# Attention with pooled keys and values: each batch's v is asked for two tiles later than its k, and one constant earlier

## The chip, the cores and the metric

One core of a Trainium2 chip runs the whole program. The metric is the device time of one execution in microseconds (us), as the median of several runs; the kernel before has 1315.34 us (three runs, 1312.93 to 1316.71). Its profiled execution took 1315.6 us, of which 1313.8 us lie between the first and the last instruction (the span).

## The reference, cut to what matters

```
def _attn_ref(q, k, v):            # 8 batches, 8 heads, 576 positions, 64 wide
    k_p = k.reshape(B, H, Sp, 8, D).mean(axis=3)      # 72 pooled keys
    v_p = v.reshape(B, H, Sp, 8, D).mean(axis=3)      # 72 pooled values
    scores = scale * np.matmul(q, k_p.transpose(0, 1, 3, 2))
    attn = exp(scores - max) / (sum + 1e-09)
    return np.matmul(attn, v_p)

x = attn_out as 4608 tokens of 512
x = _moe_ref(x, w_skip, w_gate, w1, w2)    # each token kept or sent to one of 8 experts
return _moe2_ref(x, w_in, w_out)           # (h * sigmoid(h)) @ w_out, h = x @ w_in
```

## The kernel before

The program has three stages one behind the other: the attention (up to about 150 us of the span, its last tiles up to about 175 us), the mixture of experts, and two large matmuls with a gate. The change touches the attention alone.

**Tiles.** The 4608 tokens are worked off in 36 tiles of 128. Two batches share nine tiles: `first = [0, 4, 9, 13, 18, 22, 27, 31]` is the first tile of each batch. The loop over `i` runs a software pipeline: in turn `i` it takes the scores of tile `i+2` (`s` on PE, their maximum `mx` on DVE, their exponentials `prb` on ACT), transposes those of tile `i+1` (`pt` on PE, copied to `pts` on ACT), multiplies tile `i` with the values (`pv` on PE) and divides by the sums (`post` on DVE: `sm`, `cc`, `x`, `lg`). Each finished tile `x` is written to HBM by one transfer `xa<-x`. The tiles `x` lie in a ring of four, so that the `x` of tile 7 must wait until the write of tile 3 has landed. The product `pv` has one buffer, so that the next `pv` waits until DVE has written `x`.

**What a batch needs.** Three transfers bring it: q and k (1152 KB each) and v (1200 KB, 120 partitions by 2560 numbers). DVE pools k (`kp`), ACT spreads it (`kbd`). POOL pools v in three additions, two into `v` itself and a third into `vp`, and spreads `vp` into `vex`. PE transposes `vp` (`vtp`, in `router1`), ACT copies that to `vt`, PE multiplies it with the router's weights (`cps`, in `router2`), and DVE puts the result into `vex`. For batch b+1 POOL is asked to begin two turns ahead of the batch b before it (`i + 2 == first[b]`), and `router1` stands three turns further on.

**Order.** Nothing is scheduled by a planner: each engine works its instructions in the order in which the code is written. All loads and all `xa` writes are issued by SP, in that order, on one hardware queue; SP stops at each write until DVE has finished the tile. The loads of batch b+2 are written in turn `first[b] - 2`:

```
if i + 2 == first[b]:
    if 0 < b < B - 1:
        loadq(b + 1)
        pool_k(b + 1, nc.vector, (0,))
        pool_v(b + 1)
    if b + 2 < B:
        loadk(b + 2)
        loadv(b + 2)
```

**The triangle's constants.** `constb` (64 KB) is loaded by SP in turn 2; in turn 6 `consts()` converts it on ACT to `trib`, which the routing needs.

A wrapper records every operation, so that nearly all rows of the profile name its line, L110; the operations are told apart by their tiles.

Of the kernel before, what the change touches and what calls it, by code (L numbers as in the profile page):

```python
# [18 lines left out]
P = 128  # L19
B, H, S, D = 8, 8, 576, 64  # L20
# [32 lines left out]
C_E, C_MV, C_LID, C_WT, C_THR, C_LE, C_UN, C_PK, C_TRI = 0, 2, 13, 49, 57, 153, 217, 241, 265  # L53
# [99 lines left out]
class Kern:  # L153
# [19 lines left out]
    def attention(self, xa, rs, extra):  # L173
        nc, tc, c = self.nc, self.tc, self.c
        self.todo = todo = []
        self.slow = iter(())
        with tc.tile_pool(name="as", bufs=1) as s1, \
# [11 lines left out]
            def loadk(b):  # L189
                k_t[b] = s2.tile([P, 4, G, POOL], F32, name=f"k{b}", tag="k")  # L190
                nc.sync.dma_start(k_t[b].rearrange("p a g t -> p a (g t)"), self.kT[b])

            def loadv(b):
                v_t[b] = s2.tile([P, NC, POOL, D], F32, name=f"v{b}", tag="v")
                for c in (slice(0, ON0), slice(ON0, NC)) if b == 0 else (slice(NC),):
                    nc.sync.dma_start(v_t[b][:CP, c].rearrange("p c t d -> p c (t d)"), self.vR[b][:, c])

            def loadq(b):
                q_t[b] = s2.tile([P, 4, S], F32, name=f"q{b}", tag="q", bufs=3)
                nc.sync.dma_start(q_t[b], self.qT[b])  # L200
# [15 lines left out]
            def pool_v(b, on_dve=0):  # L216

                v, g, n = v_t.pop(b), nc.gpsimd, on_dve
                vp = st[b, "v"] = s2.tile([P, NC, D], F32, name=f"vp_{b}", tag="vp")
                if n:  # L220
                    nc.vector.tensor_reduce(vp[:CP, 0:n], v[:CP, 0:n].rearrange("p c t d -> p c d t"), AX.X, ALU.add)
                v, vp = v[:CP, n:], vp[:CP, n:]
                g.tensor_tensor(v[:, :, 0:4], v[:, :, 0:4], v[:, :, 4:8], ALU.add)
                g.tensor_tensor(v[:, :, 0:2], v[:, :, 0:2], v[:, :, 2:4], ALU.add)
                g.tensor_tensor(vp, v[:, :, 0], v[:, :, 1], ALU.add)

            def values(b):
                vp, ve = st[b, "v"], vex[b % NB]
                for i, (h0, n) in enumerate(HEADS):
                    j = HOFF[i]  # L230
                    nc.gpsimd.tensor_tensor(ve[:CP, j:j + n, 0:D], bc(vp[:CP, i], 1, n),
                                            bc(mv[:CP, j:j + n], 2, D), ALU.mult)

            def keys(b):
                kp, kb = st.pop((b, "k")), kbd[b % NB]
                for j in range(2):
                    nc.scalar.mul(kb[:, :, j, :], kp, c[:, C_E + j:C_E + j + 1])

            def router1(b):
                vpf = st[b, "v"].rearrange("p c d -> p (c d)")  # L240
                ps = self.hp.tile([P, 512], F32, name=f"vtp_{b}", tag="hp")
                nc.tensor.transpose(ps[:, 0:CP], vpf[:CP, 0:128], self.ident[:CP, :CP])
                nc.tensor.transpose(ps[:, CP:2 * CP], vpf[:CP, 128:256], self.ident[:CP, :CP])
                nc.tensor.transpose(ps[:D, 2 * CP:3 * CP], vpf[:CP, 256:320], self.ident[:CP, :CP])
                vt = s2.tile([P, 3, CP], F32, name=f"vt_{b}", tag="vt")
                nc.scalar.copy(vt[:D, 2], ps[:D, 2 * CP:3 * CP])
                nc.scalar.copy(vt[:, 0:2].rearrange("p a b -> p (a b)"), ps[:, 0:2 * CP])
                st[b, "t"] = vt
# [17 lines left out]
            def scores(t):  # L266
                pr = prb[t % 2]
                mx = s2.tile([P, H], F32, name=f"mx_{t}", tag="mx")
                pss = []
                for a in range(2):  # L270
                    ps = self.hp.tile([P, 512], F32, name=f"s_{t}{a}", tag="hp")
                    for b, o, r, m in parts(t):
                        for hp in range(2):
                            nc.tensor.matmul(ps[r:r + m, 144 * hp:144 * hp + 144], q_t[b][:, 2 * a + hp, o:o + m],
                                             kbd[b % NB][:, 2 * a + hp].rearrange("p a g -> p (a g)"),
                                             start=True, stop=True)
                    nc.vector.tensor_reduce(mx[:, 4 * a:4 * a + 4],
                                            ps[:, 0:288].rearrange("p (h g) -> p h g", g=G), AX.X, ALU.max,
                                            negate=True)
                    for h in range(4):  # L280
                        nc.scalar.activation(pr[:, G * (4 * a + h):G * (4 * a + h + 1)], ps[:, G * h:G * (h + 1)],
                                             AF.Exp, bias=mx[:, 4 * a + h:4 * a + h + 1])
                return pr

            def ptrans(t, pr):
                pt = s2.tile([P, NC, P], F32, name=f"pts_{t}", tag="pts")
                for c0, n in ((0, 3), (3, 2)):
                    ps = pp.tile([P, 512], F32, name=f"pt_{t}{c0}", tag="pt", bufs=2)
                    for i in range(n):
                        nc.tensor.transpose(ps[:CP, P * i:P * (i + 1)], pr[:, CP * (c0 + i):CP * (c0 + i + 1)],  # L290
                                            self.ident)
                    nc.scalar.copy(pt[:CP, c0:c0 + n].rearrange("p c n -> p (c n)"), ps[:CP, 0:n * P])
                return pt
# [37 lines left out]
            first = [9 * (b // 2) + 4 * (b % 2) for b in range(B)]  # L331
# [27 lines left out]
            for i in range(-2, NTILE):  # L359
                if i + 2 < NTILE and i != -1:  # L360
                    prs[i + 2] = scores(i + 2)
                ready = todo.pop(0) if todo and i < NTILE - 1 else None
                if ready and ready[0]:
                    ready[0]()
                if i == -2:
                    pool_v(0, ON0)
                    values(0)
                    loadv(1)
                    loadq(1)
                if 0 <= i + 1 < NTILE:  # L370
                    pts[i + 1] = ptrans(i + 1, prs.pop(i + 1))
                if i == -1:
                    router1(0)
                    prs[1] = scores(1)
                    router2(0)
                    pool_k(1, nc.vector, (0,))
                    pool_v(1, ON1)
                    values(1)
                if i >= 0:
                    pv(i, pts.pop(i))  # L380
                a = ready[1]() if ready and ready[1] else iter(())
                b = post(i) if i >= 0 else iter(())
                for _ in range(ready[2] if ready and i < NTILE - 2 else 0):
                    next(a, None)
                for _ in b:
                    next(a, None)
                for _ in a:
                    pass
                for _ in range(SLOW):
                    next(self.slow, None)  # L390
                if i == 0:
                    pool_k(1, nc.vector, (2,))
                    keys(1)
                for b in range(B):
# [4 lines that stand above are left out]
                            pool_v(b + 1)  # L399
                        if b + 2 < B:  # L400
                            loadk(b + 2)
                            loadv(b + 2)
                    if i + 2 == first[b] + 3 + (b == 0) and b + 1 < B:
                        router1(b + 1)
                    if i + 2 == first[b] + 1 and 0 < b < B - 1:
                        pool_k(b + 1, nc.vector, (2,))
                    if i + 2 == first[b] + 2 and 0 < b < B - 1:
                        keys(b + 1)
                    if i + 2 == first[b] + 3 and 0 < b < B - 1:
                        values(b + 1)  # L410
                    if i + 2 == first[b] + 5 and b + 1 < B:
                        router2(b + 1)
                if i == 2:
                    nc.sync.dma_start(self.cb, self.con[:, P + C_TRI:])
                if i == 6:
                    self.consts()
                self.place(2 if i < 27 else 5)
                extra(i)
# [1148 lines left out]
```

## Time and profile before

| | |
|---|---|
| median of three runs | 1315.34 us |
| the profiled execution | 1315.6 us |
| its span | 1313.8 us |
| busy in the span | PE 1261.8 us (96%), DVE 852.6 (65%), ACT 569.2 (43%), POOL 358.0 (27%) |
| mean granted TensorE clock | 0.993 of full speed |
| DMA over the span | 233.77 MB, mean 178 GB/s |
| queue q1 (SP's and ACT's transfers) | 49.0% of 16 engines' span |

Busy shares are averages over three stages that differ. PE is busy nearly throughout from about 220 us on; in the attention it has gaps, and there the DMA engines are the busiest part.

### The profile page before, as it was taken

The numbers are of one execution on the slowest core, as the hardware profiler recorded it, in microseconds if no ns is written. First come the engines' busy times: TensorE is split into PE (matmuls) and PEld (weight loads), VectorE is DVE, ScalarE is ACT, GpSimd is POOL, SyncE is SP. The second block draws the span as 40 slices with busy tenths as digits, with TensorE's granted clock in tenths as the row PEclk, the third lists the DMA queues.
The fourth block names the chain that finished last, engine by engine and source line by source line (L and its number), as shares of the span: only waits on it lengthen the run. The fifth ranks groups of instructions, "written<-read, shape, count | busy, mean of one in ns | idle before, by whom it ended". The sixth has DMA issues, their size and how long they took to land.

```text
span 1313.8 us, 20408 instructions
## 1 busy us (share of the span) xinstructions
PE 1261.8 (96%) x6501; PEld 1075.2 (82%) x6502; DVE 852.6 (65%) x1553; ACT 569.2 (43%) x1188; POOL 358.0 (27%) x312
## 2 busy tenths in 40 slices
PE   6899689999989999999999999999999999999998
PEld 5788677988979898878888888788888888888887
DVE  5788676667667677779733325565784657847565
ACT  4576633454445454344433334534353333533321
POOL 4477433222123220322457503101011010111100
PEclk9999999999999999999999999999999999999999
DMA  9989535656556552248845322634356352463532
GB/s 289 295 271 275 189 126 198 201 179 201 179 190 213 198 188 84 91 167 277 296 155 211 140 93 89 224 129 167 123 183 214 137 177 94 163 210 127 176 109 92
DMA packets 94106, 233.77 MB, mean 178 GB/s; under 512 B 15068, under 2 KB 26972, under 8 KB 90375
## 3 DMA queue, kind: packets, MB, share of 16 engines
q1 hardware_dynamic: 86735, 215.82, 49.0%
q0 software_dynamic: 7008, 16.80, 3.9%
q8 instruction: 42, 0.69, 0.2%
q14 instruction: 33, 0.27, 0.1%
q10 hardware_dynamic: 288, 0.20, 0.0%
HBM read 182.58 MB, written 52.89 MB: 179 GB/s over the span
## 4 chain that ended last, share of the span: by engine, by line
PE 57%; DVE 3%; ACT 1%; issue 1%; POOL 0%; DMA 0%; DVEq 0%; ACTq 0%; POOLq 0%
PE yb L110 20%; PE ps L110 17%; PE fh L110 9%; PE fop L110 9%; PE yp L110 1%; DVE fr L110 1%; DVE ft L110 1%; PE fxp L110 0%; DVE raw L110 0%; PE sx L110 0%; DVE fgl L110 0%; DVE fsg L110 0%; DVE w2l L110 0%; ACT g L110 0%; PE hp L110 0%
## 5 line engine op out<-in xcount | busy, mean ns | idle before, releaser
L110 PE MATMUL yb<-wout,g 128*128 128x512 f32 x1152 | 268.4, 391 | 0.5 <-DMA wout<-wdo 0.4
L110 PEld LDWEIGHTS yb<-wout,g 128*128 128x128 f32 x1152 | 215.0, 188 | 45.5 <-DMA wout<-wdo 0.8
L110 POOL TENSOR_TENSOR tm<-tm,tm 128x512 f32<-128x512 f32 x24 | 32.2, 1340 | 411.9 <-ACT tm L110 411.9
L110 DVE TENSOR_TENSOR yacc<-yb,yacc 128x512 f32<-128x512 f32 x168 | 116.0, 691 | 38.4 <-PE yb L110 31.3
L110 ACT COPY tm<-ps 128x512 f32<-128x512 f32 x72 | 42.3, 588 | 146.3 <-PE ps L110 144.5
L110 PE MATMUL yp<-w2h,hh 128*128 128x512 f32 x240 | 96.4, 402 | 1.8 <-issue 0.9
L110 PE MATMUL yp<-w2l,hh 128*128 128x512 f32 x240 | 94.2, 392 | 2.2 <-DVE w2l L110 2.2
L110 PE MATMUL yp<-w2h,hl 128*128 128x512 f32 x240 | 94.4, 393 | 0.0
L110 ACT CAST g<-sg 128x512 fp32r<-128x512 f32 x96 | 59.6, 621 | 76.8 <-DVE sg L110 76.8
L110 ACT ACTIVATE hh<-hp 128x256 fp32r<-128x256 f32 (+2 forms) x96 | 41.1, 428 | 116.9 <-PE hp L110 105.8
L110 DVE TENSOR_TENSOR fsg<-fh,fsg 128x512 f32<-128x512 f32 x48 | 33.0, 688 | 80.9 <-ACT fsg L110 80.9
L110 ACT ACTIVATE prb<-s,mx 128x72 f32<-128x72 f32 x288 | 65.2, 343 | 45.7 <-DVE mx L110 44.7
L110 PE MATMUL fh<-w1l,fh 128*128 128x512 f32 x336 | 83.4, 390 | 0.0
L110 DVE TENSOR_TENSOR tm<-ps,tm 128x512 f32<-128x512 f32 x24 | 16.6, 691 | 98.1 <-PE ps L110 98.1
L110 PE MATMUL hp<-xtl,w1h 128*128 128x256 f32 (+2 forms) x384 | 71.9, 306 | 3.9 <-DVE xtl L110 3.6
L110 PE MATMUL hp<-xth,w1h 128*128 128x256 f32 (+2 forms) x384 | 71.1, 306 | 4.5 <-issue 1.7
L110 PEld LDWEIGHTS fh<-w1l,fh 128*128 128x128 f32 x336 | 62.8, 188 | 12.9
L110 DVE SCALAR_TENSOR_TENSOR hl<-hp,hh 128x256 fp32r<-128x256 f32 (+2 forms) x96 | 45.9, 478 | 39.8 <-ACT hh L110 33.1
L110 PE MATMUL hp<-xth,w1l 128*128 128x256 f32 (+2 forms) x384 | 69.7, 303 | 0.0
L110 DVE TENSOR_TENSOR g<-sg,g 128x512 fp32r<-128x512 f32 x96 | 65.7, 686 | 5.3 <-ACT g L110 4.7
L110 DVE TENSOR_TENSOR w2l<-raw,w2h 128x512 fp32r<-128x512 f32 x96 | 65.9, 692 | 3.2
L110 ACT ACTIVATE fsg<-fh 128x512 f32<-128x512 f32 x48 | 28.8, 599 | 88.3 <-PE fh L110 88.3
(230 smaller groups left out, 2780.0 us busy)
## 6 DMA issues: line engine op xcount, KB each, us to landing
raw<-w SPq DMA_DIRECT2D x88, 512.0 KB
wout<-wdo SPq DMA_DIRECT2D x48, 512.0 KB
win<-wdi SPq DMA_DIRECT2D x36, 512.0 KB
w1l<-wdi SPq DMA_DIRECT2D x36, 512.0 KB
xa<-x SPq DMA_DIRECT2D x36, 256.0 KB
fx<-xa SPq DMA_DIRECT2D x9, 1024.0 KB
v<-vR SPq DMA_DIRECT2D x7, 1200.0 KB
fr<-w_in SPq DMA_DIRECT2D x16, 512.0 KB
```

Of the source, the lines that this page charges most:

```text
L110: ins = f(*a, **k)
```

## The change

The load of v of batch b+2 moves out of the turn `first[b] - 2`, in which k's load stays, to the turn `first[b]`. For batch 2 that is a move from turn -2 to turn 0. Batches 0 and 1 are loaded ahead of the loop or in turn -2 as before. The load of `constb` moves from turn 2 to turn -2, behind the load of q of batch 1 and ahead of that of k of batch 2. No instruction is added or removed.

```
                     values(0)
                     loadv(1)
                     loadq(1)
+                    nc.sync.dma_start(self.cb, self.con[:, P + C_TRI:])
                 if 0 <= i + 1 < NTILE:
...
                         if b + 2 < B:
                             loadk(b + 2)
-                            loadv(b + 2)
+                    if i + 2 == first[b] + 2 and b + 2 < B:
+                        loadv(b + 2)
                     if i + 2 == first[b] + 3 + (b == 0) and b + 1 < B:
                         router1(b + 1)
...
-                if i == 2:
-                    nc.sync.dma_start(self.cb, self.con[:, P + C_TRI:])
                 if i == 6:
                     self.consts()
```

The first place is SP's list from the load of q of batch 1 (`q_180`) to the last write ahead of batch 3's q (`q_630`). `k_182` and `v_184` are batch 2, `q_374` is q of batch 2, `k_382` and `v_384` are batch 3; the number behind a tile is a buffer's. Before:

```order
L110 DMA q_180<-qT 128x2304
L110 DMA k_182<-kT 128x2304
L110 DMA v_184<-vR 120x2560
L110 DMA xa<-x_84 128x512 x3
L110 DMA q_374<-qT 128x2304
L110 DMA k_382<-kT 128x2304
L110 DMA v_384<-vR 120x2560
L110 DMA constb<-con 128x128
L110 DMA xa<-x_84 128x512 x5
```

And of the change (batch 2 is now `k_183` and `v_284`, its q `q_375`, batch 3 `k_383` and `v_477`):

```order
L110 DMA q_180<-qT 128x2304
L110 DMA constb<-con 128x128
L110 DMA k_183<-kT 128x2304
L110 DMA xa<-x_84 128x512
L110 DMA v_284<-vR 120x2560
L110 DMA xa<-x_84 128x512 x2
L110 DMA q_375<-qT 128x2304
L110 DMA k_383<-kT 128x2304
L110 DMA xa<-x_84 128x512 x2
L110 DMA v_477<-vR 120x2560
L110 DMA xa<-x_84 128x512 x3
```

The v of batch 2 has moved behind the write of tile 0, that of batch 3 behind the writes of tiles 3 and 4, and `constb` to the front.

The second place is SP's list for batch 4, from its k on. Before:

```order
L110 DMA k_638<-kT 128x2304
L110 DMA v_640<-vR 120x2560
L110 DMA xa<-x_84 128x512
L110 DMA xa<-lg_279 128x9x8
L110 DMA xa<-x_84 128x512 x3
```

And of the change:

```order
L110 DMA k_638<-kT 128x2304
L110 DMA xa<-x_84 128x512
L110 DMA xa<-lg_278 128x9x8
L110 DMA xa<-x_84 128x512
L110 DMA v_747<-vR 120x2560
L110 DMA xa<-x_84 128x512 x2
```

The v of batch 4 now stands behind the writes of tiles 8 and 9 and the router's logits `lg`; batches 5 to 7 follow the same pattern.

## Rows read from the trace of the kernel before

**Rows 1.** The page: the span, and shares of the chain that ended last.

```profile
span 1313.8 us, 20408 instructions
...
PE 57%; DVE 3%; ACT 1%; issue 1%; POOL 0%; DMA 0%; DVEq 0%; ACTq 0%; POOLq 0%
```

**Rows 2.** Stretches: length, busy per engine, granted clock, DMA share, GB/s.

```profile
10.00:145.00 135.00, 121.77 (x896) 107.76 (x896) 99.37 (x330) 89.70 (x361) 80.04 (x89) 0.99 0.94 290
20.00:24.00 4.00, 3.98 (x30) 3.65 (x30) 2.84 (x10) 1.77 (x10) 0.00 (x0) 1.00 1.01 215
25.00:30.00 5.00, 3.58 (x27) 3.18 (x26) 4.25 (x11) 3.62 (x15) 4.49 (x3) 1.00 0.97 404
53.00:54.00 1.00, 0.65 (x4) 0.54 (x4) 1.00 (x6) 1.00 (x7) 1.00 (x1) 1.00 0.22 78
54.00:57.00 3.00, 2.91 (x14) 2.44 (x15) 2.18 (x6) 1.94 (x9) 2.84 (x3) 0.50 0.87 265
```

**Rows 3.** PE in time order: start, us, instruction, idle time before it.

```profile
47.29 0.71 PE L110 MATMUL pt<-ident,prb 128*120 128x128 f32 x5
...
53.35 2.17 PE L110 MATMUL s<-kbd,q 128*128 128x144 f32 x8 [2.88 <-ACT prb L110]
55.31 1.27 PE L110 MATMUL pt<-ident,prb 128*120 128x128 f32 x5
...
67.83 0.71 PE L110 MATMUL pt<-ident,prb 128*120 128x128 f32 x5
...
86.14 0.74 PE L110 MATMUL pt<-ident,prb 128*120 128x128 f32 x5
...
101.88 0.71 PE L110 MATMUL pt<-ident,prb 128*120 128x128 f32 x5
```

**Rows 4.** ACT in time order, the conversion of the triangle's constants.

```profile
52.15 0.30 ACT L110 CAST trib<-constb 128x128 bf16<-128x128 f32 x1 [4.92 <-DMA constb<-con]
```

**Rows 5.** DVE in time order, the division of tile 7.

```profile
52.88 0.69 DVE L110 TENSOR_TENSOR x<-pv,sm 128x512 f32<-128x512 f32 x1 [2.63 <-DMA xa<-x]
```

**Rows 6.** SP's issues in time order (the second number runs over a whole group).

```profile
16.11 0.35 SPq L110 DMA_DIRECT2D v<-vR  x1
24.92 8.32 SPq L110 DMA_DIRECT2D xa<-x  x3
...
34.32 0.41 SPq L110 DMA_DIRECT2D v<-vR  x1
34.77 0.42 SPq L110 DMA_DIRECT2D constb<-con  x1
37.03 16.89 SPq L110 DMA_DIRECT2D xa<-x  x5
...
64.83 7.27 SPq L110 DMA_DIRECT2D xa<-x  x3
```

**Rows 7.** POOL in time order: the pooling of v, batches 2, 4 and 6.

```profile
37.04 4.52 POOL L110 TENSOR_TENSOR v<-v 120x1280 f32<-120x1280 f32 x2 [4.22 <-DMA v<-vR]
41.63 0.86 POOL L110 TENSOR_TENSOR vp<-v 120x320 f32<-120x320 f32 x1
...
72.58 2.94 POOL L110 TENSOR_TENSOR v<-v 120x1280 f32<-120x1280 f32 x1
...
79.42 0.88 POOL L110 TENSOR_TENSOR vp<-v 120x320 f32<-120x320 f32 x1
...
113.36 0.87 POOL L110 TENSOR_TENSOR vp<-v 120x320 f32<-120x320 f32 x1
```

**Rows 8.** PE in time order: transposes of the pooled v, batches 2, 4 and 6.

```profile
42.73 0.47 PE L110 MATMUL vtp<-ident,vp 120*128 120x120 f32 x3
...
81.59 0.47 PE L110 MATMUL vtp<-ident,vp 120*128 120x120 f32 x3
...
115.85 0.47 PE L110 MATMUL vtp<-ident,vp 120*128 120x120 f32 x3
```

**Rows 9.** PE in time order, a later gap.

```profile
149.97 3.05 PE L110 MATMUL pv<-vex,pts 120*128 120x148 f32 x10 [4.10 <-DVE vex L110]
```

More of the change, by code (lines that the diff above doesn't have):

```diff
@@ L369, in attention @@
                     loadq(1)
+                    nc.sync.dma_start(self.cb, self.con[:, P + C_TRI:])
                 if 0 <= i + 1 < NTILE:
@@ L401, in attention @@
                             loadk(b + 2)
-                            loadv(b + 2)
+                    if i + 2 == first[b] + 2 and b + 2 < B:
+                        loadv(b + 2)
                     if i + 2 == first[b] + 3 + (b == 0) and b + 1 < B:
@@ L412, in attention @@
                         router2(b + 1)
-                if i == 2:
-                    nc.sync.dma_start(self.cb, self.con[:, P + C_TRI:])
                 if i == 6:
```

## The prediction

> **What bounds the kernel now.** I read the page first. The chain that ended last runs back over 62% of the span, nearly all of it on PE [rows 1]. It does not reach the attention, which is where the change works. So what the attention gains is worth that much at the end only if the stages behind start earlier by the same amount; I assume they do, because they wait for its results and for no clock.
>
> Next I read the attention by stretches. From 10 to 145 us PE is busy 121.8 of 135.0 us, and the DMA engines 0.94 of the time at 290 GB/s [rows 2]: the transfers have about 8 us to spare in 135. The speed changes between two levels. While a v is under way (20 to 24 us) the queue moves 215 GB/s, while q and k are (25 to 30) 404 GB/s, both with the DMA engines busy throughout. So a v (1200 KB, 1.229 MB) holds the queue for 5.7 us, a q or k (1.180 MB) for 2.9 us, a tile's write (0.262 MB) for 0.65 us, `constb` (0.066 MB) for 0.16 us, or 0.30 us at v's rate.
>
> Then I read PE in order of time, and there one place stands out. From the `pt` at 47.29 to that at 67.83 five turns pass in 20.54 us. The same five turns two batches later, from 86.14 to 101.88, take 15.74 us [rows 3]. The attention loses **4.80 us** at this one place: PE waits 2.88 us for ACT, and then it runs with the granted clock at 0.50, the lower of its two levels (1.2 GHz), from 54 to 57 us [rows 2]; its `s` and `pt` take 2.17 and 1.27 us there.
>
> Why ACT is late stands in its row: it waited 4.92 us for `constb` [rows 4], which SP had asked for at 34.77 and which landed only at 52.15 [rows 6]. DVE was held too, by a second transfer: the `x` of tile 7 waited 2.63 us, until 52.88, for the landing of an earlier write [rows 5], by the ring of four that of tile 3, asked for at 37.03 [rows 6]. Both transfers stood behind the v of batch 3, asked for at 34.32, and that is the transfer which fills the queue at half speed. The reader should see two locks on one door: PE's next `s` needs ACT, the next `pv` needs DVE's `x`, and both let go within 0.8 us of each other. Opening one alone gives little.
>
> **The change part by part.** Nothing is added or removed; 1 load of `constb` and 6 of v (batches 2 to 7) move on SP, and nothing on the other engines.
>
> *`constb` moves ahead.* It now stands behind the q of batch 1, whose bytes run in the fast stretch from 25 us [rows 2]. ACT wants it at 52.15 - 4.92 = 47.23, some 19 us later. That lock is open.
>
> *The v of batch 3 moves behind the writes of tiles 3 and 4.* The write of tile 3 then lands 5.7 us sooner, at 52.88 - 5.7 = 47.2. DVE wants it at 52.88 - 2.63 = 50.25, so 3 us are to spare. The second lock is open too. Gain: 4.80 us, bounded below by the 2.88 us that PE stood still, above by the whole 4.80, since the undisturbed pattern is the same work. I take 4.8, because the slow clock follows from the standstill.
>
> *This v itself is later by two writes*, 1.3 us. It landed before `constb`, so before 52.15, and now at about 53.5. POOL needs 5.45 us for a `vp` (37.04 to 41.63 + 0.86) [rows 7], so it is ready at 59. PE wants it just ahead of the `pt` that stood at 67.83 and now stands near 63.7: 4 us of cover, cost nothing; without the cover it would be 1.3.
>
> *The v of batch 2 moves behind the write of tile 0.* SP asks for it not at 16.11 but behind the write at 24.92 [rows 6], 9 us later. But the queue is full from 10 us on (0.97 to 1.01 in both stretches of [rows 2]) and serves SP's list in order, so it lands later only by what now stands ahead of it: a write and `constb`, 0.65 + 0.16 to 0.30 = 0.8 to 0.95 us; at v's rate, the other bound, 1.2 + 0.3 = 1.5. POOL already waits 4.22 us for this v and ends its `vp` at 42.49 [rows 7], and PE transposes it at 42.73 [rows 8]. The cover is 0.24 us. So PE waits 0.9 - 0.24 = **0.7 us** (0.55 to 1.3). Behind `vtp` on PE stand the `s` of the next tile and all that follows, so this is lost for good.
>
> *The v of batches 4 and 6* now stand behind two tile writes and the logits. For batch 4: the write of tile 9 was asked for with the group at 64.83 [rows 6], and now at 64.83 - 4.1 = 60.7 (4.8 - 0.7 = 4.1 ahead). With 0.4 us for its issue, at most 1 us until the queue turns to it, 5.7 us under way and up to 1 us to be seen, v is there at 68.8. POOL comes to it at 72.58 - 4.1 = 68.5, so it is 0.3 us late. Its `vp` ended at 80.30 and PE used it at 81.59: 1.29 us of cover [rows 7, 8]. Batch 6 has 115.85 - 114.23 = 1.62. Below: nothing. Above, with 2 us of queue ahead of each: 1.0 + 0.7 = 1.7 us. I take **0.4** for both, near the lower end, because the covers are longer than the lateness that I get. Batches 5 and 7 have no routing work on POOL in front of `vp`; cost nothing.
>
> The queue's rate for v is where a rule and the rows part. The Trainium skill ("DMA: Bandwidth & Descriptors", "Why a DMA increments its semaphore by 16 and not by 1") says that a transfer is split over the largest number of engines up to 16 that divides its slowest dimension on both sides. For 120 partitions that makes 15 of 16, and an estimate of 404 x 15/16 = 379 GB/s or 3.2 us for a v; the trace shows 215. By that rule v4 would come 2.5 us sooner, the 0.4 would be 0, and the sum -4.1.
>
> **Sum.** -4.8 + 0.7 + 0.4 = -3.7 us. Against the profiled execution's own 1315.6 us (its span of 1313.8 and 1.8 around it) that is 1311.9. The median of the runs is 0.3 below the profiled one, so the forecast is 1311.6 us, a ratio of 0.9972. A measurement of this kernel tells about 0.3%, 3.9 us, from no change; the forecast lies on that edge.
>
> **Rivals.**
>
> *Given back to the queue.* With 0.94 of the DMA time taken, 4.8 us less for the same bytes may turn into waits for v at `vtp` in batches 2, 4 and 6: 1.3 + 1.0 + 0.7 and somewhat more, leaving about 1.5 us, 1314. For it: the spare 8 us; it would also hold if DVE or ACT had a third lock. Against it: in the empty stretch at 53 us the DMA share is 0.22 [rows 2], because SP stood still with DVE, and that hole closes with the stall.
>
> *A later gap shrinks as well.* At 149.97 PE has waited 4.10 us for `vex` on DVE [rows 9], and no row of mine says why DVE was late. If that depends on how transfers and tiles meet, another meeting may lose it: -3.7 - 4.1 = -7.8, 1307.5. Or, if it is tied to that place, it stays; this I hold for likelier, since the transfers around it move along with the tiles.
>
> *Slower: v lands later by as much as it is asked for later.* Place: PE's `vtp` of batch 2. If the landing moved by 24.92 + 0.3 - 16.11 = 9.1 us, PE would wait 9.1 - 0.24 = 8.9 us, and the sum is -4.8 + 8.9 = +4.1 at the least, 1319.4; with batches 4 and 6 late in the same way up to 1327. It decides from a landing 5 us later on. Against it: the full queue from 10 us on. The Trainium skill's rule speaks against the change here ("DMA: Bandwidth & Descriptors", "Rules for kernel authors": to overlap a transfer with compute, issue it early and wait late). The trace agrees with it only where the queue is empty.
>
> *The change doesn't do what it says*: the write of tile 3 may be held by something other than v, and DVE waits on. Then `constb` alone gives the 0.7 us between the two releases, which `vtp` takes again: 1315.
>
> **How the numbers follow.** The forecast with its spread (-2.8 to -4.7) has 0.57, given back 0.19, the later gap 0.12, slower 0.07, no effect 0.05. For 8 in 10 the range leaves out the slower rival and the upper tail of no effect, and beyond the later gap only what the bounds don't reach: 1306.5 to 1316.0; the forecast's own range is 1310.3 to 1312.8. Faster by over 0.3% (below 1311.4): 0.55 of the forecast's 0.57 share and all of the later gap, 0.43. Slower (above 1319.3): 0.06. Within: 0.51.
>
> **What would show it.** Right: ACT converts `trib` without a wait; no wait of DVE's `x` for a write; the five turns that took 20.54 us take about 15.8; the granted clock stays at full level between 50 and 60 us. `vtp` of batch 2 waits 0.5 to 1.3 us for POOL, and the `pt` that stood at 101.88 stands near 98. Wrong: a PE wait at `vtp` of over 2 us in any batch, or a POOL that begins batch 2's v after 40; or the lead of 4 us at 102 us is gone by 175, where the attention hands over.

## The result, and the profile after

The changed kernel takes 1325.64 us in the median of 6 runs (1323.41 to 1329.24), the kernel before beside it 1314.84 (6 runs): a ratio of **1.0086**, interval 1.0069 to 1.0102. It is 10.8 us slower where 3.7 us faster was forecast. Its profiled execution took 1327.84 us, 12.2 more than that of before. All rows of this section are from it.

The chain that ended last is shared out as before [rows 1]: the loss doesn't show there, because the chain again doesn't reach the attention.

```profile
span 1326.1 us, 20410 instructions
...
PE 56%; DVE 3%; ACT 1%; issue 1%; POOL 0%; DMA 0%; DVEq 0%; ACTq 0%; POOLq 0%
```

At first all goes as forecast. PE in time order (against [rows 3, 8]), then ACT (against [rows 4]):

```profile
44.27 0.53 PE L110 MATMUL vtp<-ident,vp 120*128 120x120 f32 x3 [0.83 <-POOL vp L110]
...
48.88 0.71 PE L110 MATMUL pt<-ident,prb 128*120 128x128 f32 x5
...
64.95 0.71 PE L110 MATMUL pt<-ident,prb 128*120 128x128 f32 x5
```

```profile
48.33 0.38 ACT L110 CAST trib<-constb 128x128 bf16<-128x128 f32 x1
```

`vtp` of batch 2 waits 0.83 us, `trib` waits for nothing, and the five turns that took 20.54 us take 64.95 - 48.88 = 16.07. The `pt` that stood at 67.83 stands 2.9 us earlier.

Then come two gaps that before doesn't have. DVE, PE and POOL, each in time order:

```profile
70.09 0.81 DVE L110 TENSOR_REDUCE mx<-s 128x4 f32<-128x288 f32 x2
77.53 0.17 DVE L110 TENSOR_SCALAR sm<-pv 128x8 f32<-128x8 f32 x1 [6.63 <-remote]
```

```profile
69.06 1.55 PE L110 MATMUL pv<-vex,pts 120*128 120x148 f32 x10
...
79.56 3.05 PE L110 MATMUL pv<-vex,pts 120*128 120x148 f32 x10 [5.83 <-DVE vex L110]
...
105.82 0.71 PE L110 MATMUL pt<-ident,prb 128*120 128x128 f32 x5
...
179.82 1.10 PE L110 MATMUL hp<-xth,w1h 128*128 128x384 f32 x4
```

```profile
64.77 1.07 POOL L110 DMA_INDIRECT slots<-consts,ix  x1 [5.00 <-DVE sm L110]
66.14 0.99 POOL L110 DMA_INDIRECT slots<-consts,ix  x1 [0.30 <-issue]
...
75.15 0.98 POOL L110 DMA_INDIRECT slots<-consts,ix  x1 [0.30 <-issue]
76.14 4.52 POOL L110 TENSOR_TENSOR v<-v 120x1280 f32<-120x1280 f32 x2
80.75 0.86 POOL L110 TENSOR_TENSOR vp<-v 120x320 f32<-120x320 f32 x1
```

DVE's `sm` needs the `pv` of PE that had ended by 70.61, and begins at 77.53. `remote` means that the view found no releaser near enough to name. PE then waits 5.83 us for a `vex` that stands behind this `sm` on DVE. The `pt` of [rows 3] at 101.88 stands at 105.82: a lead of 2.9 us has become a lag of 3.9. The second gap comes at 112 to 117 us, where DVE waits twice, 1.96 us and then 2.52:

```profile
117.11 0.17 DVE L110 TENSOR_SCALAR sm<-pv 128x8 f32<-128x8 f32 x1 [2.52 <-PE pt L110]
```

At the hand-over (the first matmul of the experts, `hp`, at 172.85 before) the lag is 7.0 us, at the end of the span 12.3.

The stretches of the gaps; the columns are those of [rows 2]:

```profile
70.60:77.50 6.90, 3.00 (x20) 2.17 (x18) 0.30 (x1) 2.42 (x10) 5.67 (x6) 0.88 1.00 359
75.90:82.70 6.80, 3.14 (x12) 3.10 (x13) 3.85 (x14) 1.63 (x8) 6.55 (x7) 0.50 0.34 135
...
116.80:123.60 6.80, 5.15 (x19) 4.71 (x20) 5.11 (x18) 3.33 (x13) 6.46 (x8) 0.50 0.41 165
10.00:145.00 135.00, 115.96 (x836) 102.51 (x835) 94.13 (x311) 83.43 (x333) 72.95 (x82) 0.95 0.86 266
```

In the first gap DVE works 0.30 of 6.90 us while POOL issues scatter after scatter and the DMA share is 1.00. With each gap come 6.8 us at the lower clock.

What POOL is busy with tells where to look. The nine `slots` are the scatters that write the first nine tiles into the routing table. In the kernel before, POOL's order at this place is, as the built program has it:

```
L110 DMA slots<-consts,ix_808 36864x1 x4
L110 TENSOR_TENSOR v_640<-v_640 120x5x256
L110 DMA slots<-consts,ix_808 36864x1
L110 TENSOR_TENSOR v_640<-v_640 120x5x128
L110 DMA slots<-consts,ix_808 36864x1
L110 TENSOR_TENSOR vp_881<-v_640 120x320
L110 DMA slots<-consts,ix_808 36864x1 x2
```

and in the changed kernel

```
L110 DMA slots<-consts,ix_808 36864x1 x9
L110 TENSOR_TENSOR v_747<-v_747 120x5x256
L110 TENSOR_TENSOR v_747<-v_747 120x5x128
L110 TENSOR_TENSOR vp_881<-v_747 120x320
```

In the second group four scatters in a row have become eight. The third group is nine in a row in both kernels. The diff touches no line of this. The wrapper ties each operation to the one recorded ahead of it on its engine, but a scatter consists of a register move and the transfer, and the transfer is tied to its own move, which waits for nothing. So the build is free to put scatters ahead of additions that wait for a load, and "nothing is scheduled by a planner", as the description of the kernel before has it, is wrong for them: in both kernels the additions are written ahead of seven of the nine scatters of the first group.

### The profile page after: what moved, and what is told of

It is laid out like the page before. It is cut to its first block, busy times and chain, and to the rows that moved or that the text cites. A ratio compares the mean times of both kernels' runs of the same rounds, so it can differ in the third digit from the quotient of the medians.

```text
span 1326.1 us, 20410 instructions
## 1 busy us (share of the span) xinstructions
PE 1267.1 (96%) x6501; PEld 1080.3 (81%) x6502; DVE 854.0 (64%) x1553; ACT 571.1 (43%) x1188; POOL 357.7 (27%) x312
## 4 chain that ended last, share of the span: by engine, by line
PE 56%; DVE 3%; ACT 1%; issue 1%; POOL 0%; DMA 0%; DVEq 0%; ACTq 0%; POOLq 0%
PE yb L110 20%; PE ps L110 17%; PE fh L110 9%; PE fop L110 9%; PE yp L110 1%; DVE fr L110 1%; DVE ft L110 1%; PE fxp L110 0%; DVE raw L110 0%; PE sx L110 0%; DVE fgl L110 0%; DVE fsg L110 0%; DVE w2l L110 0%; ACT g L110 0%; PE hp L110 0%
## 5 line engine op out<-in xcount | busy, mean ns | idle before, releaser
L110 PE MATMUL pv<-vex,pts 120*128 120x148 f32 (+3 forms) x400 | 61.7, 319 | 12.4 <-DVE vex L110 6.9
L110 PEld LDWEIGHTS pv<-vex,pts 120*128 120x128 f32 (+1 forms) x400 | 54.9, 190 | 16.8 <-POOL v L110 7.4
```

Source lines behind the costliest of these rows:

```text
L110: ins = f(*a, **k)
```

## The experiments

**Theory 1**: the order on POOL makes it slow, by the long runs of scatters. **Theory 2**: v is late. The kernels ran in seven sets, each on one chip; a ratio always compares with the kernel before on the same chip, and is the record's own, which differs from the quotient of the medians by up to 0.13%. Each set ran once, so chip and set can't be told apart: "a chip with the stall" below means a set of runs in which it shows.

### Each move by itself

`e1_constb_alone`: only the load of `constb` moves ahead.

> Only the load of constb moves ahead; every v is asked for where it was. POOL's order is that of the kernel before. Theory 1 (the loss comes from POOL's order: nine and eight of the routing's scatters in a row, during which TensorE's signals reach the other engines late): no loss, and a gain of 0 to 0.7 us, since DVE's wait for the write of tile 3 stays; 1314.1 to 1315. Theory 2 (the loss comes from v landing later): the same. A loss here would speak against both.

`e2_v_alone`: only the loads of v move.

> Only v moves; constb is loaded where it was. POOL's order is that of the changed kernel (nine scatters in a row, then batch 4's v; eight, then batch 6's v). Theory 1: about the time of the changed kernel, 1324 to 1328. Theory 2: the same, since v is as late. A time near 1315 would say that constb was the cause.

Measured: `constb` alone 1313.83 us, ratio 0.9989 (0.9973 to 1.0004); v alone 1327.24, ratio 1.0080 (1.0062 to 1.0097). The loss comes with the move of v, which also changes POOL's order; `constb` alone leaves that order. Both traces hold a surprise at the place of the two locks. With `constb` alone the five turns take 16.77 us, though DVE's `x` of tile 7 still waits for the write of tile 3:

```profile
52.70 0.69 DVE L110 TENSOR_TENSOR x<-pv,sm 128x512 f32<-128x512 f32 x1 [1.39 <-DMA xa<-x]
```

It hands over at 169.72, 3.1 us ahead. With v alone they take 16.45 us, and neither `trib` (48.18) nor the `x` of tile 7 (51.30) waits: the v of batch 3 then stands behind `constb` too, so this one move opens both locks.

### The order without the loads, and the loads without the order

`e3_both_moves_old_pool_order` is the changed kernel with scatters issued between the additions, and tied to the last POOL operation that isn't a scatter:

```
+                self.place(2)
                 g.tensor_tensor(v[:, :, 0:4], v[:, :, 0:4], v[:, :, 4:8], ALU.add)
+                self.place(1)
                 g.tensor_tensor(v[:, :, 0:2], v[:, :, 0:2], v[:, :, 2:4], ALU.add)
+                self.place(1)
                 g.tensor_tensor(vp, v[:, :, 0], v[:, :, 1], ALU.add)
...
+                self.tc.add_manual_dep(ins.ins, self.lead, mybir.DependencyInfo(
+                    mybir.DependencyClass.NoSync, mybir.DependencyReason.SCHED_ONLY), reason="order")
...
-                self.place(2 if i < 27 else 5)
+                self.place(0 if i in (12, 13, 21, 22) else 2 if i < 27 else 5)
```

> The changed kernel with all its loads, but POOL's order held to that of the kernel before: four scatters, v, one, v, one, vp, two, vex, one. Theory 1: the two stalls at 71 to 77 and 112 to 117 us are gone and the stall ahead of 53 us too, so the forecast comes true: 1310 to 1313. Theory 2 (late v): the loads are as late as before, so about 1325.

`e4_old_loads_nine_in_a_row` is the kernel before, tied in the same way, with each of the first two groups in one run behind `vp`:

```
-                self.place(2 if i < 27 else 5)
+                self.place(0 if i in (10, 19) else 9 if i in (11, 20) else 2 if i < 27 else 5)
```

> The kernel before with all its loads where they were, but the nine scatters of the first and of the second group in one run each, behind the batch's v and vp so that no pooling waits for them. Theory 1: two stalls of DVE of 4 to 7 us each that end 1 to 1.5 us after the last scatter of the run; 1321 to 1329. Theory 2: nothing is late, 1314 to 1316.

Measured: the loads with the old order 1316.17 us, ratio 0.9994 (0.9982 to 1.0005); the old loads with nine in a row 1328.54, ratio **1.0105** (1.0079 to 1.0130). The order alone costs as much as the whole change or more, with every load where it was. Theory 2 falls as the explanation of the loss. With the old order the loss is gone, but the gain that was expected with it (1310 to 1313 us) is not there; the part on the prediction comes back to this.

The second run of nine with the old loads, POOL, DVE, PE and ACT in time order:

```profile
117.62 1.01 POOL L110 DMA_INDIRECT slots<-consts,ix  x1 [0.15 <-issue]
...
127.93 0.98 POOL L110 DMA_INDIRECT slots<-consts,ix  x1 [0.30 <-issue]
```

```profile
121.21 0.81 DVE L110 TENSOR_REDUCE mx<-s 128x4 f32<-128x288 f32 x2
129.16 0.17 DVE L110 TENSOR_SCALAR sm<-pv 128x8 f32<-128x8 f32 x1 [7.13 <-remote]
```

```profile
121.85 1.55 PE L110 MATMUL pv<-vex,pts 120*128 120x148 f32 x10
123.24 0.47 PE L110 MATMUL vtp<-ident,vp 120*128 120x120 f32 x3
```

```profile
130.60 0.51 ACT L110 COPY vt<-vtp 64x120 f32<-64x120 f32 x2 [5.36 <-remote]
```

Nothing that POOL makes is waited for here: `vp` was ready ahead of the run, and PE transposed it at 123.24. Still DVE waits for a `pv` that PE's rows have ended at 123.40, and ACT for the `vtp` that ended at 123.71. Both go on only when the run is over (128.91). So by these rows what PE has finished reaches the engines that wait for it late, here by 5.8 us and in the first gap of the changed kernel by 6.9, while POOL issues scatters without a break. The ends of PE's rows are modelled, so the rows don't tell whether the work or only the word of it is late.

### Breaks, plain writes, small scatters

These kernels are the one with nine in a row, with additions on a scratch tile between the scatters, or other transfers in their place:

```
+            def one(j):
+                if j in BREAKS.get(g, {}):
+                    brk(BREAKS[g][j])
+                slot(j, t0 + j)
```

> The loads of the kernel before. The scatters stand behind vp as in the run with nine in a row, but a POOL addition of about 3 us on a scratch tile breaks each group: the first into 6 and 3, the second into 5 and 4, the third into 4 and 5. Theory 1 (the length of an unbroken run decides; in all stalls so far DVE stops 6 to 7 us after the first scatter of a run and goes on 0.2 to 1.5 us after the last): a stall of at most 2 us in the first group, none over 1 us in the second and third; the wait of 4.10 us ahead of 150 us shrinks to under 1 us; 1308 to 1314. If it isn't the length of the run but their number or POOL's order as such, two stalls of 4 us and more stay: 1322 and more.

> As the run before, but other breaks: the first group's scatters one by one with an addition of 160 columns (about 0.5 us) between them, the second as 3, 3, 3 with 0.9 us, the third as 3, 3, 3 with 1.5 us. Theory 1 in the form that what POOL has issued piles up faster than it is worked off: short breaks help in part, and the first group, with the same share of pause per scatter as the third, shows no more than 2 us of stall. In the form that the run must be unbroken on POOL: no stall in any group. If a break has to be long: a stall of 4 us and more in the first and second group.

For the plain writes the first group has

```
+                ins = nc.gpsimd.dma_start(self.dum[:, j:j + 1], c[:, C_LID + t:C_LID + t + 1])
```

> The kernel with nine in a row, but the nine scatters of the first group are replaced by nine plain writes of the same 128 numbers each by POOL to a scratch place (so the first nine tiles are left out of the routing table); the second group is nine scatters in a row; the third 3, 3, 3 with additions of 1.5 us between. Theory 1a (any transfer that POOL issues): a stall of 4 to 7 us in the first group as in the second. Theory 1b (the scatter with its computed addresses): none in the first, 4 to 7 us in the second. The third has none in either.

Measured on one chip: 1318.79 us, ratio 1.0055 (1.0035 to 1.0075); 1315.92, ratio 1.0032 (1.0020 to 1.0043); 1314.55, ratio 1.0027 (1.0010 to 1.0045). None has a stall in the first two groups. That would fit Theory 1 but for the control: the second group of the last kernel is nine in a row and has none either. So these three can't tell what a break does. Why they are slower than the kernel before stays open. The next two stood beside each other on one chip:

> The kernel with old loads and nine in a row once more, beside the next one on the same chip. If the stalls hang on the chip rather than on POOL's order, it is no slower here than the kernel before; if on the order, two stalls of 5 to 7 us in the first two groups and 12 us more than the kernel before.

> Nine plain writes in place of the first group's scatters (the first nine tiles are left out of the routing table), then nine scatters in a row in the second and nine in the third group. In the run with plain writes the second group, nine in a row, had no stall, against Theory 1. If that was the chip, the run with nine in a row beside it has no stall either; if it was the plain writes ahead, only this kernel is without stall in the second group; if chance, a stall of 5 to 7 us comes here.

Measured: 1326.80 us, ratio 1.0095 (1.0077 to 1.0112), and 1322.55, ratio 1.0062 (1.0039 to 1.0086). On this chip runs of nine stall in both kernels, if not all alike: DVE's longest wait is 6.74 us in the second run of the first kernel, but 2.35 in its first run, where it is split into four. The kernel with plain writes, POOL and DVE:

```profile
74.83 4.31 POOL L114 DMA_DIRECT2D dum<-consts  x8
...
121.32 0.98 POOL L114 DMA_INDIRECT slots<-consts,ix  x1 [0.30 <-issue]
```

```profile
79.05 0.17 DVE L114 TENSOR_SCALAR sm<-pv 128x8 f32<-128x8 f32 x1 [0.49 <-PE pv L114]
...
122.34 0.17 DVE L114 TENSOR_SCALAR sm<-pv 128x8 f32<-128x8 f32 x1 [6.86 <-remote]
```

The plain writes take POOL 0.54 us each and hold nobody; nine scatters on the same chip hold DVE for 6.86 us. But the plain writes end as a run after eight of them and 4.31 us, and a run of four scatters, which takes 4.9 us (67.65 to 72.58 in the kernel before), holds nobody either. So the kind of transfer and the length of the run can't be told apart by this. Four more kernels ran on a further chip:

> First group nine scatters in a row, as control; second 6 and 3, third 5 and 4, with an addition of 3 us on POOL between. Theory 1, by the length of the run (all stalls so far began 5 to 7 us after the first scatter, that is behind the fifth): a stall of 5 to 7 us in the first group, under 2 us in the second, under 1 us in the third.

> First group nine in a row, as control; second one by one with additions of 160 columns (0.5 us) between; third in pairs with additions of 320 columns (0.9 us). Theory 1 with an unbroken run as the condition: a stall of 5 to 7 us in the first group and none over 1.5 us in the others. With the rate of the scatters as the condition (they come every 1.6 us in the second group against 1.3 in a row): a stall in the second group too, shorter, of 2 to 5 us.

The edit of the next one is `ix[0:m, j:j + 1]` and `c[0:m, ...]` with `m = 32 if g == 0 else P`.

> Nine in a row in each group, but the first group's scatters have 32 rows in place of 128 (the other 96 tokens of each of the first nine tiles are left out of the routing table). If the work per row holds up the others, the first group has no stall over 2 us, the second one of 5 to 7 us. If it is the number of scatters, both have one of 5 to 7 us, or of nine times what a scatter of 32 rows takes less 6 us.

> The kernel before, for its trace on the chip of these runs: the wait of 4.10 us ahead of 150 us behind nine scatters in a row is here too, by Theory 1; if it isn't, and the first group of the runs beside it doesn't stall either, the chips differ in it.

Measured, one run each: 1314.26, 1317.12, 1313.18 and 1312.47 us, beside 1311.27 for the kernel before. No run of nine stalls here in any of the four kernels (DVE's longest wait in one is 1.42 us), that of 32 rows (0.86 us a scatter) no more than the full ones. So the stall hangs on the chip, or on what else sets these runs apart, as well as on the order, and these four tell nothing of its length or rows. The kernel before, PE ahead of 150 us (against [rows 9]):

```profile
150.12 0.76 PE L110 MATMUL s<-kbd,q 128*128 128x144 f32 x4 [1.08 <-ACT prb L110]
```

Behind the same nine scatters PE waits 1.08 us here where it waited 4.10.

### The third group broken

Two versions that were to beat both kernels: `constb` ahead, the old order on POOL, the third group as 3, 3, 3 with additions between (1.3 us each in the trace); `f1` moves the v of batch 3 too.

> constb ahead, and of the v loads only that of batch 3 is moved; POOL's order in the first two groups held to that of the kernel before; the third group, nine scatters in a row in both kernels, broken as 3, 3, 3 by additions of 1.5 us. Theory 1 (long runs of scatters hold up DVE): the gain of 4.8 us at 48 to 65 us and another 4 to 6 us at 143 to 153 us, where the kernel before waits 4.10 us and then runs 3.4 us at the lower clock: 9 to 11 us ahead at the hand-over at 175 us, 1304 to 1309 if the stages behind keep it. Theory 2 (the later v): 1311 to 1315, with the third wait as it was.

> As the run before, with every v asked for where the kernel before has it. Theory 1: 7 to 9 us ahead at the hand-over (2.8 of it from constb, as in the run with constb alone), 1306 to 1311. Theory 2: about 1314.

Measured on the chip of the run with nine in a row once more: 1313.61 us, ratio 0.9990 (0.9976 to 1.0003), and 1312.90, ratio 0.9992 (0.9980 to 1.0003). No kernel of this study is faster than the kernel before by more than the measurement tells. The first of the two hands over at 166.38, 6.5 us ahead of the trace of before, which is from another set, and ends 0.3 us behind it. The wait of [rows 9] is smaller:

```profile
146.40 0.76 PE L114 MATMUL s<-kbd,q 128*128 128x144 f32 x4 [1.79 <-ACT prb L114]
```

With `constb` alone and the third group unbroken it is 2.11 us on another chip with the stall, so this wait alone doesn't show what the break does. DVE's rows do: on the chip of these two kernels its longest wait in the third group is 1.78 and 1.79 us, for ACT, where the group is broken, and 2.60 and 3.22 us, for PE, in the two kernels of the section before that leave it nine in a row. So the broken group doesn't stall on a chip with the stall; the times don't resolve what that is worth.

### The changed kernel on a chip without the stall

> The changed kernel once more. On a chip with the stall (the kernel before at 1315 and more): 10 to 12 us slower than before, DVE idle for over 6 us in the first group. On a chip without it (the kernel before at 1311 to 1313): the lead of 4 us from the first stall is there, but POOL comes to batch 4's v only behind nine scatters, so at 76 us in place of 72.6 - 3; its vp ends at 81.6 where PE wants it at 78.5, a wait of 3 us at vtp, and as much in batch 6 behind eight: 0 to 3 us slower than before. If neither the stall nor these waits come, it is 3 to 4 us faster, as forecast.

This came on a chip with the stall: 1324.87 us, ratio 1.0082 (1.0064 to 1.0101), DVE's wait 6.64 us at 77.71. The next two ran on a chip without it:

> As before: on a chip with the stall 10 to 12 us slower than the kernel before, DVE idle for over 6 us in the first group; on a chip without it 0 to 3 us slower, with a wait of some 3 us at vtp of batches 4 and 6.

> Both moves with the old order on POOL: no stall in the first two groups on any chip. On a chip with the stall level with the kernel before, as the first time (0.9994); on one without it level or up to 4 us faster, and 3 to 6 us faster than the changed kernel.

Measured: the changed kernel 1316.45 us, ratio **1.0027** (1.0016 to 1.0038); both moves with the old order 1311.52, ratio 0.9994 (0.9984 to 1.0004). POOL and PE of the changed kernel, then PE with the old order:

```profile
75.84 0.98 POOL L110 DMA_INDIRECT slots<-consts,ix  x1 [0.30 <-issue]
76.83 4.53 POOL L110 TENSOR_TENSOR v<-v 120x1280 f32<-120x1280 f32 x2
81.44 0.86 POOL L110 TENSOR_TENSOR vp<-v 120x320 f32<-120x320 f32 x1
```

```profile
82.35 0.53 PE L110 MATMUL vtp<-ident,vp 120*128 120x120 f32 x3 [2.92 <-POOL vp L110]
...
120.78 0.74 PE L110 MATMUL vtp<-ident,vp 120*128 120x120 f32 x3 [2.35 <-POOL vp L110]
```

```profile
79.61 0.53 PE L110 MATMUL vtp<-ident,vp 120*128 120x120 f32 x3 [0.89 <-POOL vp L110]
...
115.29 0.53 PE L110 MATMUL vtp<-ident,vp 120*128 120x120 f32 x3 [0.93 <-POOL vp L110]
```

So the new order has a second price, which shows where the stall is away: batch 4's additions stand behind nine scatters and batch 6's behind eight, and PE waits 2.92 and 2.35 us for them. In the trace of the changed kernel with the stall PE doesn't wait for `vp` there (`vtp` of batch 4 at 85.53): it comes to it later than POOL.

## Why the prediction was wrong

**The step that failed** is "1 load of `constb` and 6 of v (batches 2 to 7) move on SP, and nothing on the other engines", and in the description before it "Nothing is scheduled by a planner". The build orders the scatters, and the later loads made it put them ahead of the additions of batches 4 and 6. That the order is chosen by when v is expected is likely, since moving `constb` alone leaves it as it was; it was not shown in another way. The prediction read the order on SP, where the change is written, and not on the engine that uses what is loaded. In its place the runs show a price of the order alone of 1.05% (1.0079 to 1.0130) with the old loads, and none (0.9994) for the moved loads when the old order is held.

**The two locks.** Right as to the places: both waits are gone, the clock stays at the full level from 50 to 60 us (1.00), and the five turns take 16.07 us (15.8 said). Wrong that "opening one alone gives little": `constb` alone brings 20.54 - 16.77 = 3.77 us and v alone 20.54 - 16.45 = 4.09 of the 4.47. The 4.8 was also read from one trace at the upper end: in the eleven traces with the old loads these turns take 17.5 to 20.6 us (17.51 with the breaks between, 17.95 and 20.14 in the two of nine in a row), with both moves 15.9 to 16.3.

**The v of batch 2**: 0.7 said (0.55 to 1.3), 0.83 measured at `vtp`, and 1.25 in the later trace without the stall. The full queue is borne out: SP asks for this v at 25.88, 9.8 us later than before, and POOL begins it only 1.7 us later (38.76 against 37.04). The five turns begin 1.6 us later than before (48.88 against 47.29); about half a us of that is there at 41 us already, where executions of unchanged loads differ by over a us.

**The v of batches 4 and 6**: 0.4 said, at most 1.7. With the old order it is 0.82 + 0.91 us on one chip and 0.89 + 0.93 on another, just above the upper bound: on the second chip POOL waits until 71.88 for batch 4's v, 3 us later than the 68.8 worked out. The write of tile 9 is asked for at 61.92 there, not at 60.7, because the lead is under 3 us and not 4.1, and from it to POOL's start 10.0 us pass where 8.1 were allowed; no run shows the two allowances of 1 us in them one by one. By the rule of the Trainium skill that the prediction set against the rows ("DMA: Bandwidth & Descriptors", "Why a DMA increments its semaphore by 16 and not by 1") this term would be 0; the waits side with the rows.

**The sum at the hand-over** then comes near where the order is held: with both moves and the old order the first `hp` stands 4.0 us earlier with the stall (168.89 against 172.85) and 2.4 us without (167.21 against 169.65), where 3.7 was said; the traces compared are from different sets.

**That the lead lasts to the end** was assumed and is not so. From the hand-over to the end of the span:

| kernel | hand-over, us | from there to the end |
|---|---|---|
| before, two chips | 172.85, 169.65 | 1140.9, 1141.1 |
| changed, three sets (the last without the stall) | 179.82, 181.14, 174.07 | 1146.3, 1142.6, 1140.9 |
| `constb` alone | 169.72 | 1142.7 |
| both moves, old order, two chips | 168.89, 167.21 | 1146.3, 1142.4 |
| `constb`, v of batch 3, third group broken | 166.38 | 1147.7 |
| old loads, nine in a row | 184.55 | 1142.8 |

The stages behind take 1140.9 to 1147.7 us for the same work. Each row is one execution, and the runs of one kernel spread by 3 to 9 us, so single differences in the last column are not the kernel's alone; the medians say the same, though: 4.0 us of lead at the hand-over, 0.8 us in the time (1316.17 against 1316.93), and 2.4 and 1.0 without the stall (1311.52 against 1312.53). A part of it can be the clock. Stretches of before, then of both moves with the old order on the chip with the stall (columns of [rows 2]):

```profile
180.00:230.00 50.00, 44.98 (x257) 39.69 (x256) 37.19 (x102) 20.21 (x44) 14.48 (x13) 0.97 0.51 174
...
370.00:400.00 30.00, 24.54 (x186) 22.87 (x185) 22.48 (x43) 16.75 (x34) 8.86 (x8) 1.00 0.72 241
```

```profile
180.00:230.00 50.00, 44.70 (x244) 39.20 (x243) 35.68 (x93) 17.74 (x40) 14.36 (x14) 0.93 0.47 157
...
370.00:400.00 30.00, 25.66 (x168) 23.50 (x167) 21.13 (x40) 15.86 (x32) 8.20 (x7) 0.89 0.66 222
```

The mean clock is lower by 0.04 of 50 us and by 0.11 of 30, which is 2.0 + 3.3 = 5.3 us of full clock, against the 5.4 by which this kernel falls back behind the hand-over. The waits of PE in these stretches are alike in both traces, 1.4 to 2.8 us; after one of them the clock falls, in the other trace it doesn't. The changed kernel's first trace falls back by 5.4 us there too, its second by 1.6. Without the stall the clock explains nothing: in the same stretches before has 0.97 and 0.94, both moves with the old order 0.97 and 1.00, and yet the latter falls back by 1.3 us. This was seen and not tried by an experiment of its own, and why the lead is lost stays open.

**The changed kernel's loss** in its first trace, then: a lead of 2.9 us turned by the first gap into a lag of 3.9, by the second into more, 7.0 at the hand-over after the old wait near 150 us, which costs less here (2.50 us) than before, and 5.4 behind it. Of the rivals, the slower one named the time (1319 to 1327) and not the cause: POOL begins batch 2's v at 38.76, before the 40 that it would have taken. The later gap, for which "no row of mine says why DVE was late", has its likely reason: it stands behind the third group, nine scatters in a row from 136.13 to 148.22, and DVE waits for PE's work there:

```profile
146.42 0.17 DVE L110 TENSOR_SCALAR sm<-pv 128x8 f32<-128x8 f32 x1 [3.30 <-PE pt L110]
```

On the chip without the stall DVE's longest wait behind the same nine is 1.37 us.

## What to carry to other kernels

Before costing a move of loads, set the built order of *every* engine before and after beside each other, above all of the engine that waits for the load; the build may put an operation that waits for nothing ahead of one that waits, and pinning it is a line. Long runs of scatters from POOL belong broken up among its other work, behind what others wait for: runs of at most four stalled nobody in the traces here; how short a run has to be was not found. And a few us won early are worth what the stages behind leave of them: read the lead at the hand-over and at the end apart.

## What the runs showed of the hardware

**Long runs of scatters from POOL hold up those who wait for PE, in some sets of runs.** In four of the seven sets DVE's longest wait in or right behind a run of eight or nine scatters, 1.28 us apart, is 2.35 to 7.13 us in each of the 20 such runs traced; in the other three it is at most 1.43 in 11 runs, and runs of at most four show no more than 1.8 in either; the kernel before takes 1314.3 to 1316.9 us on the former and 1311.3 to 1312.5 on the latter (its runs beside the timed kernels). DMA traffic isn't needed for it: while DVE waits 3.30 us in the third group of the kernel before, the DMA share is 0.05 (columns of [rows 2]):

```profile
144.00:148.00 4.00, 1.78 (x13) 1.33 (x12) 1.39 (x5) 2.10 (x6) 3.09 (x4) 1.00 0.05 9
```

What differs between the chips, how long a run has to be, and by which path it acts stay open. The Trainium skill ("SBUF — State Buffer", "SBUF: two separate sides") states that among the engines only DVE and GpSimd contend, for one pair of ports under an exclusive lock, and that PE and ACT wait for no one. By that rule DVE alone would be held; the row of `vt` above shows ACT waiting 5.36 us in the same stretch for what PE's rows have finished, so the lock alone does not explain it.

**Plain writes are cheap beside scatters**: those of 128 numbers took POOL 0.54 us each, against 0.98 us and 0.30 between for a scatter.
